# The last attention step: GpSimd subtracts the last head's probability remainders before three scatters instead of between them

## The chip, the cores and the metric

One core of a Trainium2 chip runs the whole kernel. Its engines work in parallel: TensorE (PE, with its weight loads as PEld), VectorE (DVE), ScalarE (ACT) and GpSimd (POOL); SyncE (SP) and GpSimd also issue DMA transfers. The metric is the device time of one execution in microseconds. Three runs of the kernel before gave 763.99, 764.95 and 767.49 us, so its median is 764.95 us.

## What is computed

Eight batches of eight attention heads (576 positions, 64 dimensions) are followed by a mixture of eight experts that picks one expert per token. Cut to what matters:

```python
scores = scale * np.matmul(q, k.transpose(0, 1, 3, 2))          # 8 x 8 heads, causal
bias = -(cum[:, :, :, None] - cum[:, :, None, :])               # from the running sum of s
scores = np.where(causal, -1000000000.0, scores + np.minimum(bias, 0.0))
attn = np.exp(scores - np.max(scores, axis=-1, keepdims=True))
attn = attn / (np.sum(attn, axis=-1, keepdims=True) + 1e-09)
x = np.matmul(attn, v)                                          # all heads of a token: 512 columns
...
expert_idx = np.argmax(logits, axis=1)                          # of normalised x and embeddings
for e in range(E):
    mask = expert_idx == e
    h = np.maximum(x[mask] @ w1[e], 0.0)
    out[mask] = gate_w[mask, None] * (h @ w2[e])
```

## The kernel before, in words

The attention part goes head by head, n = 0 to 63, one call of `step(n)` each. For a head TensorE computes the scores into the PSUM tiles `ta` and `tb`; ScalarE takes their exponentials into the f32 tile `P` (lines 498 and 501, columns 0 to 576 and 576 to 1600). A product in 16-bit needs each probability in two parts: the high one is the upper half of the f32 word, and the remainder `PL = P - high` is a subtraction that `pl_` writes, on GpSimd (helper `psub`, line 252) or, in some steps, partly on VectorE (line 508). `pv(n)` then multiplies high and remainder with the values into the one PSUM bank `om`: three matmuls per block, lines 526 to 528, of which line 528 reads `PL`. `norm1`, `norm2` and `norm3` (lines 539, 543 and 551, VectorE) divide and copy `om` into the token rows `xt`; the next `pv` writes `om` again and so waits for line 551.

`pv` runs one to two heads behind the scores. In the last step, n = 63, it has reached head 61; `pv` of heads 62 and 63 stand behind the loop, as does the second half of the last head's remainders.

When a batch of eight heads is done, its router ranks the tokens by expert, and five indirect DMAs (`scat`, line 670, called through `scatter()` from the queue `scats`) write the rows `xt` to the DRAM table `xs`, which is sorted by expert. GpSimd issues them. The five of batch 6, the batch preceding the last, stand in the last steps. Behind them GpSimd issues a gather `xload(0, 2)` (line 739), which reads the third tile of expert 0's rows back from `xs`; it waits for the last of these scatters to land. TensorE transposes the gathered tile in `xtr(0, 2)` (line 767).

TensorE does not wait for that: `first_pass(m)` (matmuls of line 903) multiplies the first 256 gathered rows with the eight 128-column pieces of expert 0's first weights. Behind the loop the order on TensorE is `pv(62)`, `first_pass(0)`, `pv(63)`, `first_pass(1)` to `first_pass(4)`, then `xtr(0, 2)` and `first_pass(5)` to `first_pass(7)`. The weights are made 16-bit in two parts as well: ScalarE writes the high part (line 875) and VectorE the low one (`wlow`, line 883, from two tiles in SBUF). Each `wlow` lets SP load another piece of weights (line 826).

The order on each engine is the order of the code: a manual schedule, in which an engine works through its own list and waits at semaphores. So the order of the calls in `step` and behind the loop is the order on GpSimd. Behind the loop stands:

```python
    for n in range(3, NH):
        step(n)
    pl_(NH - 1, 576, 1600, "p")
    while scats:
        scatter()
    xload(0, 2)
    pv(NH - 2, range(5))
    norms(NH - 2)
    wsq(15)
    wlow(1)
    first_pass(0)
    wsq(16)
    wlow(1)
    pv(NH - 1, range(5))
```

Of the kernel before, what the change touches and what calls it, by code (L numbers as in the profile page):

```python
# [31 lines left out]
SCN = [1, 1, 0, 0, 0, 0, 2, 1]  # L32
# [82 lines left out]
def main(ctx, tc, qkh, qkc, vtin, s_in, emb, tau, w1h, w2h, out, shared, nb):  # L115
# [36 lines left out]
    NH, LA = nb * H, 5  # L152
# [69 lines left out]
    def setup4():  # L222
        t = p2.tile([128, DM], F32, tag="lT", name="idx", bufs=1)
        for i, n in enumerate(("recf", "gp", "va", "gi", "tmp")):
            IX[n] = t[:, 40 * i:40 * i + 40].rearrange("p (b j) -> p b j", j=5)
        IX["cnt0"], IX["va0"], IX["gi0"] = t[:, 200:202], t[:, 202:205], t[:, 205:208].bitcast(I32)
        IX["gi"], IX["recf"], IX["va"], IX["va0"] = (IX[n].bitcast(I32) for n in ("gi", "recf", "va", "va0"))
        nc.gpsimd.iota(IX["recf"], pattern=[[S, 8], [128, 5]], base=0, channel_multiplier=1)
        nc.gpsimd.iota(IX["tmp"].bitcast(I32), pattern=[[NT, 8], [128, 5]], base=0, channel_multiplier=1)
        nc.gpsimd.tensor_copy(IX["gp"], IX["tmp"].bitcast(I32))  # L230
        IX["L"], IX["T"], IX["w"] = t[:, 284:324], t[:, 324:364], t[:, 364:369]
        IX["r"], IX["E"] = t[:, 224:244], t[:, 244:284]
        IX["WS"], IX["RS"], IX["SB"] = t[:, 432:434], t[:, 434:434 + 2 * NE], t[:, 450:454].bitcast(BF16)
        IX["SQ"] = t[:, 454:470].rearrange("p (k j) -> p k j", k=2)
        IX["b1"], one = t[:, 208:208 + NE], t[:, 216:216 + NE].bitcast(I32)
        nc.gpsimd.iota(one, pattern=[[NT, NE]], base=1, channel_multiplier=0)
        nc.gpsimd.tensor_copy(IX["b1"], one)
        zr = t[0:NE, 284:284 + XR // 4].bitcast(I32)
        nc.gpsimd.memset(zr, 0)
        for k in range(4):  # L240
            o = slice(XR // 4 * k, XR // 4 * (k + 1))
            nc.sync.dma_start(xs.rearrange("(e n) c -> e n c", e=NE)[:, 0, o], zr)
            nc.sync.dma_start(xs[0:SPM].rearrange("(t p) c -> t p c", p=128)[SPL // 128 - 1:, 127, o], zr[0:2])

    def setup3():
        nc.gpsimd.tensor_copy(base, ebase)
        nc.gpsimd.tensor_scalar(wsel, base, -1.0 / NT, float(NE), op0=ALU.mult, op1=ALU.add)
        nc.gpsimd.tensor_copy(wval, wsel.unsqueeze(1).to_broadcast([128, 5, NE]))
        nc.gpsimd.memset(wval[64:128, 4:5], 0.0)
# [4 lines left out]
    def load(g, o=slice(0, QW + KW)):  # L254
        if g >= NGg:
            return
        qkb = qkbs[g % 3]
        if g > 0:
            nc.gpsimd.dma_start(qkb[0:64, o], qkh[g][:, o], **(dict(max_dma_last_dim=4864) if g < 3 else {}))
        G[g] = dict(QB=qkb[:, 0:QW].rearrange("p (h s) -> p h s", h=HG), KB=qkb[:, QW:].rearrange("p (h s) -> p h s", h=HG))  # L260

    def loadc(g):
        if g == 1:
            for i in range(2):
                nc.gpsimd.dma_start(qkbs[1][64 + i:65 + i, QW:].bitcast(F32), chl[HG:2 * HG, i, :].bitcast(F32))
        elif 1 < g < NGg:
            nc.sync.dma_start(qkbs[g % 3][64:66, QW:].bitcast(F32), cumd[:, HG * g:HG * (g + 1), :].rearrange("x r s -> x (r s)").bitcast(F32))
# [45 lines left out]
    def hset(g):  # L313
        if g < NGg:
            for h in range(HG):
                HD.setdefault(HG * g + h, {}).update(QC=QCs[g % 2][:, h], KC=KCs[g % 2][:, h])
# [152 lines left out]
    def ta_(n, m):  # L469
        assert MP.get(("ready", n // 2))  # L470
        t = HD[n]["ta"] = ps_t.tile([128, 1024], F32, tag="t", name="ta")
        mask(t[:, 256:512], tri0, start=True)
        s1(m)
        hh_(n, t[:, 256:512], 0, 0, 256)
        hh_(n, t[:, 512:832], 0, 256, 576, True)
        hl_(n, t[:, 512:832], 0, 256, 576, True)
        hl_(n, t[:, 256:512], 0, 0, 256, True)
# [52 lines left out]
    def norm1(n):  # L530
        if n not in HD:
            return
        b, hh = n // H, n % H
        o = HD[n]["o"]
        if hh == 0:
            XT[b] = p2.tile([128, 5, XR], F32, name="xt", bufs=2)
        z = HD[n]["z"] = p2.tile([128, 5], F32, name="z")
        ov = HD[n]["ov"] = o[:, 0:365].rearrange("p (j c) -> p j c", c=73)
        nc.vector.tensor_scalar(z, ov[:, :, 72 * (hh % 2)], 1.0e-9 * 2.0 ** PSH, 2.0 ** XSH, op0=ALU.add, op1=ALU.mult)

    def norm2(n):
        if n in HD:
            nc.vector.reciprocal(HD[n]["z"], HD[n]["z"])
# [489 lines left out]
    def fslot():  # L1033
        while first:
            first.popleft()()  # L1035
# [151 lines left out]
    def step(n):  # L1187
        m = n + LA - (n < 6)
        live = n < NH
        b0, b1, c8 = n // H, n // H + 1, n % H  # L1190
        prev = n - 1 < NH
        g, c = n // HG, n % HG
        if live and c == 0:
            hset(g + 1)
            if n > 4:
                load(g + 2)
                loadc(g + 2)
        if n == 10:
            setup4()
            setup3()  # L1200
        fslot()
        norm1(n - 3)
        if live:
            ta_(n, m)
        if prev:
            pl_(n - 1, 576, PS(n), "p")
        sr(m, 3)
        norm2(n - 3)
        sa(m)
        if live:  # L1210
            expa(n)
            prep(n, True)
        norm3(n - 3)
        if NH - 7 < n < NH:
            brk[0] = False
            slots(4)
        if live:
            tb_(n)
        sr(m, 2)
        if live and n % 2 == 0:  # L1220
            tbm(n)
        s3(m)
        if live:
            if n % 2:
                tbm(n)
            tbl(n)
        if n < NH - 6 or n >= NH:
            mslot()
        if prev and PS(n) < 1600:
            pl_(n - 1, PS(n), 1600, "v")  # L1230
        if n < NH:
            wlow(1)
        k = n - NH + 8
        if k == 3:
            wsq(8, True)
        if n < NH - 1:
            emm(n)
        sb(n, m)
        sbr(m)
        if n < NH:  # L1240
            tail(n)
        if n == 5:
            s1(10)
            sr(10, 3)
            s2(10)
        if n == 7:
            vscale(1)
        pv(n - 2, [0, 1, 2])
        if n == 7:
            fslot()  # L1250
        if rq:
            rq.popleft()()
        if n == 5:
            sr(10, 2)
            sr(10, 1)
            s3(10)
        pv(n - 2, [3, 4])
        if n == NH - 1:
            emm(n)
        if n == 5:  # L1260
            s4(10)
        if NH - 7 < n < NH:
            mslot()
        if n >= NH - 1:
            for f in (norm1, norm2, norm3):
                f(n - 2)
        if live:
            expb1(n)
            if k == 7:
                wsq(13)  # L1270
            vcp(n, False)
        if k == 3:
            wsum(0)
        aslot()
        if n == 4:
            load(3)
            loadc(3)
        if live:
            prep(n, False)
            vcp(n, True)  # L1280
        if n == NH - 1:
            xcv(0, 0)
            xtr(0, 1, pxs())
            xcv(0, 1)
        if k > 0:
            wsq((0, 2, 5, 8, 9, 10, 11, 14)[k])
            wcv((0, 0, 0, 0, 2, 1, 2, 1, 1, 1, 0)[k], True)
        brk[0] = False
        if n < NH - 6:
            slots(4)  # L1290
        if n in (4, 5, 6):
            vsq(1, ((0,), (1, 2), (3,))[n - 4])
        if H <= n < NH and 2 <= c8 < 6 and b1 < nb:
            vsq(b1, (c8 - 2,))
        if live and c8 == 6 and 1 < b1 < nb:
            vscale(b1)
        if n == 3:
            loadt(1, pair(1))
        if H <= n < NH and c8 < 4:
            loadt(b1, c8)  # L1300
        if n == NH - 9:
            wissue(3)
        for _ in range(SCN[c8] if n < NH - 22 else 2 if NH - 3 < n < NH else 1 + (c8 > 5) + 4 * (n > NH - 6)):
            scatter()
        later()
        if live and c == 0:
            addl(g + 1, True)
        if live and c == 1:
            addl(g + 1, False)
        mrow1(m)  # L1310
        if live:
            pl_(n, 0, 576, "p")

    def PS(n):
        return 1024 if NH - 7 < n < NH - 1 else 1600
# [390 lines left out]
```

## Time and profile before

| | |
|---|---|
| median of three runs | 764.95 us (763.99 to 767.49) |
| profiled execution, its own time | 763.98 us |
| its span, first to last instruction | 762.3 us |
| busy: PE / DVE / ACT / POOL | 97% / 70% / 75% / 52% of the span |
| PE waits over 0.15 us between 335 and 375 us | 0.18, 0.92, 0.34 and 5.94 us |

A busy share is an average over the whole span. The change is in one stretch of it, from about 335 to 351 us, where the attention part ends and the experts begin; there it is the single waits of the engines that count, and the time at which each comes. A row of the timeline gives the start in us from the span's start, the duration in us, the engine, the line, the operation, what it writes and reads, its shape, and in brackets the idle time of the engine before it with what ended it. The time of a transfer is not in the row of its issue: a DMA row gives the time that the engine took to issue it.

### The profile page before, as it was taken

How to read it: one execution, taken by the hardware profiler on the slowest of the kernel's cores; microseconds unless marked ns; L12 is line 12 of the kernel's file. 1: busy time of each engine (PE TensorE's matmuls, PEld its weight loads, DVE VectorE, ACT ScalarE, POOL GpSimd, SP SyncE). 2: the span in 40 equal slices, each digit the busy share in tenths (PEclk: the TensorE clock that was granted, in tenths of full speed). 3: DMA queues.
4: the chain of work that ended last, by engine and by line, in shares of the span. 5: the costliest groups of instructions: out<-in, count | busy, mean ns of one | idle time of the engine just before them, and what ended most of it. 6: DMA issues, size and time to landing. Idle time of an engine off the chain costs nothing. (4 is left out here: it accounts for less than half of the span.)

```text
span 762.3 us, 20951 instructions
## 1 busy us (share of the span) xinstructions
PE 739.1 (97%) x7992; PEld 536.4 (70%) x7992; DVE 530.2 (70%) x1818; ACT 568.2 (75%) x1029; POOL 397.2 (52%) x376
## 2 busy tenths in 40 slices
PE   7999999999999999999689999999999999999996
PEld 4889999999999999998365455545444554554554
DVE  8778888888888888898467767655665566745621
ACT  9898989898989998986377867837648578475410
POOL 9997898989897989693422113222221122312011
PEclk9999999999999999999899999999999999999999
DMA  7789879797979796874525956845755668553001
GB/s 151 175 193 191 173 180 204 180 207 168 216 172 210 181 215 155 174 256 132 172 89 168 207 171 194 159 139 152 181 171 141 177 186 186 169 130 100 13 15 58
DMA packets 76003, 124.01 MB, mean 163 GB/s; under 512 B 38824, under 2 KB 39232, under 8 KB 75033
## 3 DMA queue, kind: packets, MB, share of 16 engines
q0 software_dynamic: 19632, 69.69, 39.4%
q1 hardware_dynamic: 56260, 52.84, 25.9%
q8 instruction: 71, 1.16, 0.7%
q14 instruction: 40, 0.32, 0.1%
HBM read 93.99 MB, written 21.49 MB: 151 GB/s over the span
## 5 line engine op out<-in xcount | busy, mean ns | idle before, releaser
L252 POOL TENSOR_TENSOR PL<-P 128x576 f16<-128x576 f32 (+2 forms) x128 | 205.6, 1726 | 13.1 <-ACT P L498 8.6
L903 PE MATMUL pe<-xH,wt 128*128 128x512 f16 (+1 forms) x576 | 153.1, 344 | 0.5 <-PEq L1008 0.5
L982 POOL DMA_INDIRECT out<-Kx,xj x39 | 43.2, 1108 | 195.0 <-DVE Kx L981 164.5
L903 PEld LDWEIGHTS <-wt 128*128 128x128 f16 x960 | 86.0, 98 | 80.8 <-issue 1.5
L526 PE MATMUL om<-vh,P 128*128 128x73 f16 x960 | 106.9, 199 | 0.5 <-DVE sc L1035 0.3
L528 PE MATMUL om<-vh,PL 128*128 128x73 f16 x960 | 106.1, 197 | 0.9 <-POOL PL L252 0.9
L527 PE MATMUL om<-vl,P 128*128 128x72 f16 x960 | 106.3, 196 | 0.0
L739 POOL DMA_INDIRECT Qx<-xs,idx x40 | 46.5, 1163 | 108.3 <-ACT vjunk L838 41.3
L362 PE MATMUL s<-qkb 96*128 96x288 f32 (+4 forms) x272 | 96.2, 368 | 2.0 <-DVE M L370 0.9
L903 PE MATMUL pe<-xL,wt 128*128 128x512 f16 (+1 forms) x288 | 96.0, 344 | 0.0
L527 PEld LDWEIGHTS <-P 128*128 128x128 bf16 x960 | 94.7, 99 | 0.9 <-issue 0.5
L528 PEld LDWEIGHTS <-PL 128*128 128x128 f16 x960 | 93.8, 98 | 1.0 <-POOL PL L252 1.0
L526 PEld LDWEIGHTS <-P 128*128 128x128 bf16 x960 | 93.8, 99 | 0.6 <-DVE xt L551 0.4
L905 PE MATMUL pxs<-xH,wt 128*128 128x64 f16 x432 | 83.2, 193 | 0.0
L370 DVE CUSTOM_DVE_ANT_0 junk<-s,mS 128x448 bf16<-128x448 f32 (+3 forms) x144 | 73.9, 520 | 5.0 <-PE s L362 3.1
L974 PE MATMUL pxs<-wt,hq 128*128 128x512 f16 x297 | 74.0, 384 | 0.0
L501 ACT ACTIVATE P<-tb 128x1024 f32<-128x1024 f32 x64 | 65.2, 1018 | 3.0 <-PE tb L467 1.9
L974 PEld LDWEIGHTS <-hq 128*128 128x128 f16 x360 | 35.5, 99 | 42.7 <-issue 1.7
L905 PEld LDWEIGHTS <-wt 128*128 128x128 f16 x648 | 63.5, 98 | 0.4
L464 PE MATMUL tb<-QC,KC 128*128 128x448 f32 (+3 forms) x256 | 63.4, 307 | 0.0
L460 PE MATMUL tb<-qkb 128*128 128x448 f32 (+3 forms) x256 | 61.1, 286 | 0.0
L883 DVE SCALAR_TENSOR_TENSOR wt<-ring,idx,wt 128x512 f16<-128x512 f32 x80 | 56.8, 745 | 4.7 <-ACT wt L875 4.6
(328 smaller groups left out, 1997.3 us busy)
## 6 DMA issues: line engine op xcount, KB each, us to landing
qkb<-qkh POOLq DMA_DIRECT2D x15, 1216.0 KB, 8.9
ring<-w2h SPq DMA_DIRECT2D x44, 256.0 KB
ring<-w1h SPq DMA_DIRECT2D x36, 256.0 KB
KC<-qkh POOLq DMA_DIRECT2D x14, 576.0 KB, 8.5
QC<-qkh POOLq DMA_DIRECT2D x14, 576.0 KB, 9.1
vT<-vtin SPq DMA_DIRECT2D x24, 320.0 KB
rw<-w1h SPq DMA_DIRECT2D x15, 256.0 KB
rw<-w2h SPq DMA_DIRECT2D x12, 256.0 KB
```

The lines of the kernel that those rows point to most:

```text
L252: nc.gpsimd.tensor_tensor(out, a, b_, op=ALU.subtract)
L362: nc.tensor.matmul(out, G[g]["QB"][0:96, h, 128 * i:128 * i + 128], G[g]["KB"][0:96, h, lo:hi], start=True, stop=True)
L370: nc.vector.tensor_tensor_reduce(out=jk, in0=src, in1=ms, scale=1.0, scalar=NEG, op0=ALU.add, op1=ALU.max, accum_out=MP[n // 2][:, n % 2, ...
L460: nc.tensor.matmul(out, G[g]["KB"][:, h, ks:ks + 128], G[g]["QB"][:, h, 64 + qlo:64 + qhi], start=start, stop=False)
L464: nc.tensor.matmul(out, HD[n]["KC"][:, ks:ks + 128], HD[n]["QC"][:, qlo:qhi], start=False, stop=stop)
L501: nc.scalar.activation(HD[n]["P32"][:, 576:1600], HD[n]["tb"], AF.Exp, scale=0.125)
L526: nc.tensor.matmul(out, lh, vh[:, kb], start=(kb == 0), stop=False)
L527: nc.tensor.matmul(out[:, u:u + 72], lh, vl[:, kb], start=False, stop=False)
L528: nc.tensor.matmul(out, ll, vh[:, kb], start=False, stop=(kb == j))
L903: nc.tensor.matmul(h, w[:, 128 * c:128 * c + 128], x[:, c, lo:hi], start=(c == 0 and k == 0), stop=(c == 3 and k == 2))
L905: nc.tensor.matmul(X["a"][:, HALF * m:HALF * m + HALF], w[:, 128 * c:128 * c + 128], x[:, c, hi:hi + HALF], start=(c == 0 and k == 0), sto ...
L974: nc.tensor.matmul(y, h, w, start=(m == 0 and k == 0), stop=(m == 7 and k == 2))
```

## The change

In step n = 63 the loop that calls `scatter()` no longer runs, where it ran twice before; in step 62 it still runs twice. The two scatters stay in the queue `scats`, and the `while scats` behind the loop now issues three instead of one, after both halves of the last head's remainders.

```diff
-        for _ in range(SCN[c8] if n < NH - 22 else 2 if NH - 3 < n < NH else 1 + (c8 > 5) + 4 * (n > NH - 6)):
+        for _ in range(SCN[c8] if n < NH - 22 else 2 if n == NH - 2 else 0 if n == NH - 1 else 1 + (c8 > 5) + 4 * (n > NH - 6)):
             scatter()
```

On GpSimd the list changes in one place, the last step of the attention part. `PL2` and `P322` belong to head 62, `PL0` and `P320` to head 63; `xs` is the table in DRAM, `Qx` the tile that the gather fills.

```order
 L252 TENSOR_TENSOR PL2_112<-P322_88 128x576
 L252 TENSOR_TENSOR PL2_112<-P322_88 128x1024
-L670 DMA xs_61<-xt_5631,pos_6704 36864x580 x2
-L252 TENSOR_TENSOR PL0_110<-P320_86 128x576
-L252 TENSOR_TENSOR PL0_110<-P320_86 128x1024
-L670 DMA xs_61<-xt_5631,pos_6704 36864x580
+L252 TENSOR_TENSOR PL0_110<-P320_86 128x576
+L252 TENSOR_TENSOR PL0_110<-P320_86 128x1024
+L670 DMA xs_61<-xt_5631,pos_6704 36864x580 x3
 L739 DMA Qx_6608<-xs_61,idx_1290 128x580
 L554 COPY xt_6488<-idx_1290 128x5x4
```

The two subtractions of head 63 move up past two scatters, and now follow those of head 62 directly; all three scatters stand together ahead of the gather.

VectorE's list is the same before and after. Around the same place it holds these rows (the first `L883` is the `wlow` of step 63; the first three rows behind it are the norm of head 61, the next three that begin with `L539` the norm of head 62):

```order
L883 SCALAR_TENSOR_TENSOR wt<-rw_177,idx,wt 128x512
L539 TENSOR_SCALAR z<-om 128x5
L543 RECIPROCAL z<-z 128x5
L551 TENSOR_TENSOR xt<-om,z 128x5x72
L311 SCALAR_TENSOR_TENSOR vl<-V,sc,vh_109 128x2x144
L777 TENSOR_TENSOR rv<-pxs,xH 128x4x128 x2
```

Nothing moves in it; what changes is which of GpSimd's instructions run beside it.

## Rows read from the trace of the kernel before

**Rows 1.** The page: span, and busy time of each engine.

```profile
span 762.3 us, 20951 instructions
PE 739.1 (97%) x7992; PEld 536.4 (70%) x7992; DVE 530.2 (70%) x1818; ACT 568.2 (75%) x1029; POOL 397.2 (52%) x376
```

**Rows 2.** Waits, 325 to 374 us: total, times, longest, in us.

```profile
PE om L528 <- POOL PL L252: 0.9, 1, 0.9
PE pxs L767 <- DMA Qx<-xs,idx: 0.3, 1, 0.3
```

**Rows 3.** Timeline of PE: heads 62 and 63, the passes, both transposes.

```profile
339.81 0.21 PE L526 MATMUL om<-vh,P 128*128 128x73 f16 x1 [0.18 <-DVE xt L551]
...
342.78 0.20 PE L526 MATMUL om<-vh,P 128*128 128x73 f16 x1
...
344.13 0.21 PE L528 MATMUL om<-vh,PL 128*128 128x73 f16 x1 [0.92 <-POOL PL L252]
...
350.55 0.27 PE L903 MATMUL h<-xH,wt 128*128 128x256 f16 x1
...
351.16 0.30 PE L767 MATMUL pxs<-ident,Qx 128*128 128x128 f32 x1 [0.34 <-DMA Qx<-xs,idx]
...
374.39 0.48 PE L767 MATMUL pxm<-ident,Qx 128*128 128x128 f32 x1 [5.94 <-DMA Qx<-xs,idx]
```

**Rows 4.** Timeline of POOL: remainders of heads 62 and 63, three scatters, gather.

```profile
335.30 1.18 POOL L252 TENSOR_TENSOR PL<-P 128x576 f16<-128x576 f32 x1
336.40 1.92 POOL L252 TENSOR_TENSOR PL<-P 128x1024 f16<-128x1024 f32 x1
338.49 1.26 POOL L670 DMA_INDIRECT xs<-xt,pos  x1 [0.17 <-issue]
340.06 0.98 POOL L670 DMA_INDIRECT xs<-xt,pos  x1 [0.31 <-issue]
341.05 3.02 POOL L252 TENSOR_TENSOR PL<-P 128x576 f16<-128x576 f32 x2
344.24 1.20 POOL L670 DMA_INDIRECT xs<-xt,pos  x1 [0.17 <-issue]
347.49 1.04 POOL L739 DMA_INDIRECT Qx<-xs,idx  x1 [2.05 <-DMA xs<-xt,pos]
```

**Rows 5.** Timeline of ACT: the last exponential of head 63.

```profile
336.76 1.02 ACT L501 ACTIVATE P<-tb 128x1024 f32<-128x1024 f32 x1 [0.25 <-POOL PL L252]
```

**Rows 6.** Timeline of DVE: three low weights, and one norm copy.

```profile
330.17 1.64 DVE L883 SCALAR_TENSOR_TENSOR wt<-rw,idx,wt 128x512 f16<-128x512 f32 x1
...
335.78 3.10 DVE L883 SCALAR_TENSOR_TENSOR wt<-rw,idx,wt 128x512 f16<-128x512 f32 x1
...
341.94 0.53 DVE L551 TENSOR_TENSOR xt<-om,z 128x360 f32<-128x360 f32 x1
342.39 2.23 DVE L883 SCALAR_TENSOR_TENSOR wt<-wt,idx 128x512 f16<-128x512 f32 x1
```

**Rows 7.** Timeline of POOL: earlier remainders, one alone and two in a row.

```profile
317.03 0.94 POOL L252 TENSOR_TENSOR PL<-P 128x448 f16<-128x448 f32 x1 [1.08 <-ACT P L501]
...
329.74 1.52 POOL L252 TENSOR_TENSOR PL<-P 128x576 f16<-128x576 f32 x1 [0.40 <-ACT P L498]
331.22 1.38 POOL L252 TENSOR_TENSOR PL<-P 128x448 f16<-128x448 f32 x1
```

**Rows 8.** Timeline of SP: the first of three weight loads from 338.94.

```profile
338.94 0.33 SPq L826 DMA_DIRECT2D rw<-w1h  x1
```

**Rows 9.** Timeline of POOL: the last of five later scatters, and its gather.

```profile
364.44 0.99 POOL L670 DMA_INDIRECT xs<-xt,pos  x1 [0.30 <-issue]
370.93 1.05 POOL L739 DMA_INDIRECT Qx<-xs,idx  x1 [5.50 <-DMA xs<-xt,pos]
```

**Rows 10.** Windows: busy by engine and instructions, TensorE clock, DMA share, GB/s.

```profile
344.50:347.50 3.00, 3.00 (x53) 2.78 (x50) 2.96 (x11) 0.57 (x2) 0.95 (x2) 1.00 0.28 68
363.00:369.50 6.50, 5.45 (x26) 2.25 (x23) 5.17 (x28) 2.79 (x10) 2.12 (x2) 1.00 0.83 277
```

## The prediction

> **What bounds the kernel now.** I read the page first: TensorE is busy for 97% of a span of 762.3 us [rows 1], so time is won or lost only where TensorE waits or starts to wait. The list of waits for the stretch around the change comes next, and shows two kinds that touch it [rows 2]: one wait of line 528 for GpSimd's remainders, and one of the transpose, line 767, for the gathered tile. The timeline of TensorE puts them in order [rows 3]. pv(62) starts at 339.81, released by VectorE's norm of head 61. pv(63) starts at 342.78, stops almost at once, and goes on at 344.13, after an idle 0.92 us that GpSimd's last subtraction ended. The passes then run without a gap up to 350.55 + 0.27 = 350.82, and the transpose waits 0.34 us for the gather and starts at 351.16. The reader is to see that the two waits are 7 us apart, and that nothing but TensorE's own work lies between them.
>
> GpSimd's timeline says why each ends when it does [rows 4]. The remainders of head 63 start at 341.05, after two scatters, and end at 344.07. The third scatter starts at 344.24, the gather 3.25 us later, at 347.49, when that scatter has landed, and TensorE's transpose 3.67 us after the gather's start. So both waits hang on the same engine, and the change shortens one by moving work that stands ahead of the other.
>
> **The change, part by part.**
>
> The subtractions. Nothing else holds them back: the second exponential of head 63 ends at 336.76 + 1.02 = 337.78 [rows 5], before GpSimd has finished head 62 at 336.40 + 1.92 = 338.32 [rows 4]. The two take 3.02 us together, so undisturbed they end at 338.32 + 3.02 = 341.3, and pv(63) at 342.78 finds them ready. The stop in pv(63) goes: about 1.0 us (0.92 us of idle time in the row, and a few matmul slots of a tenth beside it).
>
> The scatters. Their number and the number of subtractions ahead of the gather are the same as before. Undisturbed the third would start 341.3 + 0.17 after the subtractions, then two intervals as before: 340.06 - 338.49 = 1.57 for the first and 0.98 + 0.31 = 1.29 for the second, at 344.3 against 344.24 [rows 4]. The gather then stays where it was, within 0.1 us.
>
> The neighbour on VectorE. A low weight of line 883 starts at 335.78 and takes 3.10 us; it ends 0.56 us after GpSimd's 338.32. The one at 342.39 ends at 344.62, 0.55 us after GpSimd's 344.07 [rows 4, 6]. So line 883 makes no progress beside a subtraction of GpSimd, while the norm copy of line 551 at 341.94 keeps its 0.53 us. In the changed list the first of them finds another subtraction waiting at 338.3 where there was a scatter. The rows show both outcomes of such a meeting. At 330.17 line 883 waits for a subtraction that ends at 331.26, gets in ahead of the next, which stands in the row from 331.22 and takes 1.38 us instead of 0.94, and ends at 331.81 [rows 6, 7]. At 336.40 the next subtraction came first, and VectorE waited through both [rows 4, 6].
>
> I take the first outcome, since the two rows overlap by 0.04 us where VectorE got in and by 0.08 us where it did not (335.30 + 1.18 against 336.40), and the boundary at 338.3 has a wide subtraction in front, whose successor is the narrower one, as at 331.2 the successor was narrow. It is one case each, so I keep the other as a rival. The price of the first is 1.38 - 0.94 = 0.44 us on GpSimd: the subtractions end at 341.3 + 0.44 = 341.7, still a microsecond before pv(63), and the third scatter starts at 344.75, 0.5 us later than before. With 3.25 and 3.67 us behind it as before, the transpose starts at 344.75 + 6.92 = 351.67 instead of 351.16.
>
> The Trainium skill states a rule for this meeting (SBUF — State Buffer, Who interferes with whom): VectorE and GpSimd share one pair of ports as an exclusive lock, a VectorE instruction with two SBUF inputs needs it, and whoever issues first has it for the whole instruction. By that rule VectorE, waiting since 335.78, would get the pair at the first boundary, and the slow outcome could not occur. The row of 3.10 us disagrees, since it spans two subtractions, and the measurement decides: both outcomes stay open.
>
> What is late next. TensorE arrives at the transpose 1.0 us earlier, at 349.8, and the tile arrives 0.5 us later: it waits 1.8 us there instead of 0.34. All of the gain is given back there, and 0.5 us more. From then on everything hangs on TensorE: the passes 5 to 7, and behind them the ranks and the scatters of the last batch. So the 5.94 us at 374.39 [rows 3] absorb nothing, because the gather that ends them comes later by the same amount.
>
> The sum: -1.0 for the stop in pv(63), +1.0 for the earlier arrival at the transpose, +0.5 for the later gather: +0.5 us. Against the profiled execution's own 763.98 us that is 764.5. The median of the runs is 0.97 us above that execution, so 765.5 us as a median of runs. From below, with VectorE's turn free, the term is +0.1; from above it is the first rival.
>
> **The rivals.**
>
> VectorE is shut out through both pairs, and the kernel gets slower. Place: the boundary at 338.3. If GpSimd's next subtraction comes first there, as it did at 336.40, and again at 339.4, line 883 ends at 341.3 + 0.56 = 341.8 instead of 338.88, 2.95 us later. Behind it in VectorE's list stands the norm of head 61, and pv(62) waits for that: 342.76 instead of 339.81. The stop of pv(63) is gone, so TensorE is 2.95 - 1.0 = 1.95 us late, ends the passes at 352.8, finds the tile landed, and is 1.6 us behind 351.16: 766.6. The three weight loads from 338.94 [rows 8] follow line 883 and move into the scatters' time, which can add another 1.0 us. It decides from the point at which line 883 ends more than 1.9 us later than now. For it: the row of 3.10 us; against it: the row of 1.64 us. Should VectorE get in at 339.4, between the two subtractions of head 63, the norm is 1.1 us late, the removed stop pays for that, and the sum stays at +0.5.
>
> The three scatters hinder each other. The last of five scatters in a row starts at 364.44, and the gather behind it at 370.93, 6.5 us later against 3.25 here [rows 4, 9]. If three in a row cost as much, the transpose comes another 3.25 us later, +3.8 in all: 768.7. Against it: DMA was busy for 0.83 of the time there and for 0.28 behind the third scatter here [rows 10], and the weight loads that fill the difference are not issued in this place.
>
> The stop goes and most of it stays gone. This needs the gather to land a microsecond earlier than now, or the tile not to be needed; the row of the transpose with its 0.34 us shows that it was already the later of the two, so at most 0.3 us is free of that condition. For it: two of GpSimd's idle gaps beside scatters could close, 0.17 and 0.31 us. Price: -0.3 to -1.0, so 764.0 to 764.7.
>
> The change does not do what it says, because the subtractions wait for the exponential: excluded by 337.78 against 338.32, down to a delay of 0.5 us of ScalarE.
>
> **How the numbers follow.** The forecast, given back at the transpose with +0.1 to +0.8, has a chance of 0.58; VectorE shut out 0.21; scatters that hinder each other 0.09; a gain kept 0.09; anything else 0.03. The predicted time is 765.5 us. The forecast's own range is 764.2 to 767.0, since a median of three runs of this kernel moves by more than its term: the runs before lie between 763.99 and 767.49. With the shut-out VectorE at 766.6 to 767.6 and half of the kept gain, the range is 763.4 to 768.1. About 0.5%, 3.8 us here, is what a measurement of this kernel can tell from no change: faster would be below 761.1 and slower above 768.8. No case reaches the first, and the scatters' case reaches the second only with some help. So 0.02 faster, 0.94 within, 0.04 slower.
>
> **What would show it.** Right: line 528 of head 63 without a wait for GpSimd; line 883 ending near 338.9; the third scatter near 344.7 and the gather near 348.0; TensorE's wait at the transpose grown from 0.34 to about 1.8 us. The first rival shows as a row of line 883 of about 6 us and a wait of 3 us at the first matmul of pv(62), with almost none at the transpose; the second as a gather that starts over 5 us after the third scatter; the third as a transpose that starts before 351. A time below 763 or above 768.8 would make the prediction wrong as a whole.

## The result: slower by 0.6%, outside the predicted range

| | us |
|---|---|
| predicted | 765.5 (763.4 to 768.1) |
| after, median of five runs | 771.61 (771.43 to 772.53) |
| before, median of five runs in the same comparison | 766.24 (763.99 to 767.49) |
| ratio, 95% interval | 1.0063 [1.0046, 1.0080] |
| the same comparison on another chip | 1.0044 [1.0027, 1.0061] |

Medians and ratios here and below are over the fast executions; two that were far slower, 1056.04 us of before and 4257.9 us of before with one low weight put off, are left out.

The profiled execution of after took 771.61 us. Its page, beside [rows 1]: the span is 7.5 us longer, TensorE is busy 4.2 us longer (at a lower clock, as will be seen), and VectorE 4.2 us longer with the same 1818 instructions.

```profile
span 769.8 us, 20951 instructions
PE 743.3 (97%) x7992; PEld 539.1 (70%) x7992; DVE 534.4 (69%) x1818; ACT 568.0 (74%) x1029; POOL 395.5 (51%) x376
```

The waits of TensorE from 325 to 374 us of after (total, times, longest), beside [rows 2]: the stop of line 528 and the wait at the transpose are both gone, and a new wait of 4.9 us stands where there was none, at line 526.

```profile
PE om L526 <- DVE xt L551: 4.9, 1, 4.9
PE V L300 <- DVE vl L311: 0.4, 1, 0.4
PE om L526 <- DVE base L641: 0.3, 1, 0.3
```

TensorE's timeline of after, beside [rows 3]. The wait is at the first matmul of pv(61), one head earlier than any place the prediction spoke of. pv(62) starts at 347.67 and pv(63) at 350.62, without a stop. The row of 357.41 is the third tile's transpose, which starts without a wait, 6.25 us later than before.

```profile
337.49 0.60 PE L767 MATMUL pxs<-ident,Qx 128*128 128x128 f32 x4
...
343.00 0.22 PE L526 MATMUL om<-vh,P 128*128 128x73 f16 x1 [4.92 <-DVE xt L551]
...
346.82 1.01 PE L767 MATMUL pxs<-ident,Qx 128*128 128x128 f32 x4
347.67 0.20 PE L526 MATMUL om<-vh,P 128*128 128x73 f16 x1
...
350.62 0.20 PE L526 MATMUL om<-vh,P 128*128 128x73 f16 x1
...
357.41 0.60 PE L767 MATMUL pxs<-ident,Qx 128*128 128x128 f32 x4
```

GpSimd's timeline of after, beside [rows 4]. The four subtractions are one row now, 5.97 us without a pause, and end at 340.95; the third scatter is 0.28 us earlier than before, and its gather follows 5.87 us later instead of 3.25.

```profile
333.99 0.99 POOL L670 DMA_INDIRECT xs<-xt,pos  x1 [0.30 <-issue]
334.98 5.97 POOL L252 TENSOR_TENSOR PL<-P 128x576 f16<-128x576 f32 x4
341.12 1.26 POOL L670 DMA_INDIRECT xs<-xt,pos  x1 [0.17 <-issue]
342.68 0.98 POOL L670 DMA_INDIRECT xs<-xt,pos  x1 [0.30 <-issue]
343.96 0.93 POOL L670 DMA_INDIRECT xs<-xt,pos  x1 [0.30 <-issue]
349.83 1.04 POOL L739 DMA_INDIRECT Qx<-xs,idx  x1 [4.93 <-DMA xs<-xt,pos]
```

VectorE's timeline of after, beside [rows 6], says what TensorE waited for. The low weight of **step 62** starts at 334.70 and takes 6.81 us: it ends 0.56 us after the last of the four subtractions. Behind it stands the norm of head 60, whose copy of line 551 releases pv(61). The low weight of step 63, about which the prediction was, comes at 342.87 and takes 0.74 us.

```profile
334.70 6.81 DVE L883 SCALAR_TENSOR_TENSOR wt<-rw,idx,wt 128x512 f16<-128x512 f32 x1
341.43 0.66 DVE L311 SCALAR_TENSOR_TENSOR vl<-V,sc,vh 128x432 f16<-128x432 f32 x1
342.01 0.15 DVE L539 TENSOR_SCALAR z<-om 128x5 f32<-128x5 f32 x1
342.19 0.19 DVE L543 RECIPROCAL z<-z 128x5 f32<-128x5 f32 x1
342.42 0.53 DVE L551 TENSOR_TENSOR xt<-om,z 128x360 f32<-128x360 f32 x1
342.87 0.74 DVE L883 SCALAR_TENSOR_TENSOR wt<-rw,idx,wt 128x512 f16<-128x512 f32 x1
```

Two windows of after (columns as in [rows 10]) show the second part of the price: after the wait began, TensorE's granted clock was 0.50 of full speed, 1.2 instead of 2.4 GHz, for 6.83 us, and once more for 3.42 us after a 1.91 us wait at 401.6. The execution before had a wait of 1.83 us in that later place, too, but no fall of the clock behind it.

```profile
340.82:347.65 6.83, 4.65 (x53) 4.60 (x53) 3.65 (x10) 0.58 (x2) 3.30 (x4) 0.50 0.68 199
402.26:405.68 3.42, 3.42 (x9) 1.18 (x8) 2.66 (x18) 2.70 (x7) 0.00 (x0) 0.50 0.29 87
```

**The sum against the profile of before.** The transposes of the first and second gathered tile start 2.52 us apart before (336.51 and 339.03) and 9.33 apart after. Of the 6.81 more, 4.92 is the wait, and the other 1.9 the halved clock. The first transpose itself was 0.98 us late already. Behind that 1.54 us are saved, the stop (about 1.0) and the waits at the transpose (0.34) and at pv(62) (0.18), so the third tile is 0.98 + 6.81 - 1.54 = 6.25 us late. The rest of the 7.5 us of span comes later, with the second fall of the clock: the two transposes around it (401.57 and 408.96) stand 7.39 us apart, the same two 5.70 us in before (395.73 and 401.43). That fall cannot be put down to the change. The same two transposes are 7.38 us apart in before with both low weights put off, and 5.70 in after with a memset added (both follow below).

The 0.98 us are not the change's doing. They arise at 325.1, ten microseconds ahead of the first moved instruction, where VectorE's share of a remainder (line 508) meets a subtraction of GpSimd. The timelines of VectorE and GpSimd there, first of before, then of after:

```profile
325.13 0.74 DVE L508 TENSOR_TENSOR PL<-P 128x576 f16<-128x576 f32 x1
...
322.49 4.17 POOL L252 TENSOR_TENSOR PL<-P 128x448 f16<-128x448 f32 x3
```

```profile
325.13 1.53 DVE L508 TENSOR_TENSOR PL<-P 128x576 f16<-128x576 f32 x1
...
322.50 3.54 POOL L252 TENSOR_TENSOR PL<-P 128x448 f16<-128x448 f32 x3
```

In the one profile of before VectorE went first (0.74) and GpSimd waited; here GpSimd went first and VectorE took 1.53. In all twelve other profiles of this study it went as here. TensorE then waits 0.34 us at line 526 (for line 641) and 0.41 us at line 300 (for line 311), both for VectorE, where it did not wait in the first profile of before; that is most of the 0.98 us.

### The profile page after: what moved, and what is told of

The parts are those of the page before. It is cut to its first block, busy times and chain, and to the rows that moved or that the text cites. A ratio compares the mean times of both kernels' runs of the same rounds, so it can differ in the third digit from the quotient of the medians.

```text
span 769.8 us, 20951 instructions
## 1 busy us (share of the span) xinstructions
PE 743.3 (97%) x7992; PEld 539.1 (70%) x7992; DVE 534.4 (69%) x1818; ACT 568.0 (74%) x1029; POOL 395.5 (51%) x376
## 5 line engine op out<-in xcount | busy, mean ns | idle before, releaser
L883 DVE SCALAR_TENSOR_TENSOR wt<-ring,idx,wt 128x512 f16<-128x512 f32 x80 | 56.8, 745 | 4.8 <-ACT wt L875 4.8
```

## The experiments

The theory: VectorE's line 883 has two inputs in SBUF and makes no progress beside a subtraction of GpSimd, nor at the boundary between two of these that follow each other directly. A scatter between the pairs ended its wait; the change took that scatter away. Rivals: that the three scatters together make the time, or the clock alone. Starts are those of the transposes of tiles 0 to 3 on TensorE.

| kernel | line 883, step 62 / 63 | longest wait, tile 0 to 1 | starts of tiles 0, 1, 2, 3 | span | median; ratio to before |
|---|---|---|---|---|---|
| before, first profile | 0.74 / 3.10 | none | 336.51, 339.03, 351.16, 374.39 | 762.3 | 766.24 |
| before, second profile | 3.87 / 0.74 | 1.99 | 338.20, 343.94, 354.52, 378.49 | 768.0 | 769.58; 0.9992 |
| after | 6.81 / 0.74 | 4.92 | 337.49, 346.82, 357.41, 380.76 | 769.8 | 771.61; 1.0063 |
| after, second profile | 6.81 / 0.74 | 4.91 | 337.58, 346.92, 357.50, 380.95 | 770.1 | 770.39; 1.0044 |
| after, one scatter between | 3.87 / 3.10 | 1.98 | 338.47, 344.64, 355.34, 379.34 | 768.4 | 769.48; 1.0012 |
| after, memset between | 6.86 / 0.74 | 4.96 | 338.25, 347.07, 357.61, 381.12 | 770.9 | 773.67; 1.0050 |
| after, both low weights late | none there | none | 337.77, 340.28, 352.78, 375.89 | 763.2 | 765.36; 0.9985 |
| before, both low weights late | none there | none | 338.03, 340.54, 353.09, 375.94 | 765.0 | 765.87; 0.9986 |

Before was run beside each set: 768.51 for the first (35 runs), 766.98 for the second (29), 769.75 for the third (20) and 766.91 for the last (22). Its times differ by nearly as much between the sets as the effect asked for, so the ratios are what is compared. One difference between the sets shows in the traces: every profile of the first and third sets has a wait of 2.51 to 3.78 us at line 974 for line 883, and no other profile has it. What makes it was not tried.

**First set: does it hang on the low weights, on the scatter or on the clock?** Both low weights of steps 62 and 63 are put off to a place behind pv(63), in after and in before. This changes part of the computation: a few low parts of expert 0's first weights are made from raw weights that the next ones have already replaced.

```diff
-        if n < NH:
+        if n < NH - 2:
             wlow(1)
...
-    wlow(4)
+    wlow(6)
```

> The changed kernel, with the low weights of steps 62 and 63 (line 883, two tiles in SBUF as inputs) put off until after the attention steps, so that none of them stands beside the four subtractions. Lock theory (VectorE's instruction waits as long as GpSimd's subtractions follow each other, and the norm of head 61 waits behind it): TensorE's wait of 4.92 us at pv(61) falls below 0.5 us, its clock stays at 2.4 GHz around 341 to 348 us, and the time is 763 to 766.5 us, about 5 to 8 us below the changed kernel. Scatter theory (three scatters in a row make the gather late, and that costs the 5 us): the gather still starts 5.9 us after the third scatter, and the time stays at 770 to 772.

> The kernel before, with the low weights of steps 62 and 63 put off in the same way: what the putting off is worth by itself. Lock theory: before loses little to the lock, since a scatter separates the two pairs of subtractions; the stop of 0.92 us in pv(63) stays, and the time is 763 to 766. A theory in which the putting off itself is worth the 5 us: 760 to 762.

After with this took 771.16 us, ratio 1.0030 [1.0013, 1.0048]; before with it 769.44, 1.0005 [0.9990, 1.0021]. Both times miss the lock theory's ranges, and that of after lies in the scatter theory's. The place did what the lock theory says: in after the first two transposes stand 2.51 us apart, the wait of pv(61) is gone, and the gather starts 2.98 us after the third scatter, not 5.9. In before the stop in pv(63), which I expected to stay, did not come; TensorE waited 1.57 us at pv(62) instead. Passes on TensorE waited for low weights (0.35 and 0.48 us at line 903, 3.75 and 3.78 at line 974, all for line 883). The waits at line 903 stand in these two kernels alone; that at line 974 is the one of the whole set, so the putting off makes at most a part of it. After also had a wait of 2.55 us at pv(63), ended by the norm of head 62; what held that norm its records leave open. By the total the test is inconclusive; the second set mends it.

One scatter goes back between the pairs:

```diff
-2 if n == NH - 2 else 0 if n == NH - 1 else
+2 if n == NH - 2 else 1 if n == NH - 1 else
```

> The changed kernel with one of the three scatters back between the subtractions of head 62 and those of head 63; two follow behind. Lock theory: VectorE gets in at that scatter, the low weight that waited 6.81 us waits at most 4 us, and the time is 764 to 768. Scatter theory: two scatters in a row instead of three delay the gather by a third less, 769 to 770.5.

It took 769.48 us, 1.0012 [0.9994, 1.0031]: by the ratio most of the loss is gone. The time itself lies in the range of the scatter theory; the ranges were set from 766.24 us for before, which took 768.51 in this set. In the timelines of VectorE and GpSimd line 883 of step 62 ends 0.56 us after the first pair, beside the scatter that follows, and takes 2.94 us less than in after; that of step 63 then waits beside the second pair. The gather starts 6.32 us after the second of the two scatters (5.87 after the third of three in after), so the scatter theory fails here.

```profile
335.69 3.87 DVE L883 SCALAR_TENSOR_TENSOR wt<-rw,idx,wt 128x512 f16<-128x512 f32 x1
...
340.91 3.10 DVE L883 SCALAR_TENSOR_TENSOR wt<-rw,idx,wt 128x512 f16<-128x512 f32 x1
...
335.98 3.02 POOL L252 TENSOR_TENSOR PL<-P 128x576 f16<-128x576 f32 x2
339.17 1.26 POOL L670 DMA_INDIRECT xs<-xt,pos  x1 [0.17 <-issue]
340.45 3.00 POOL L252 TENSOR_TENSOR PL<-P 128x576 f16<-128x576 f32 x2
```

The clock by itself: 22 matmuls without use fill TensorE's wait in after.

```diff
+        if n == NH - 1:
+            for _ in range(22):
+                w = wt(1, 0)[0]
+                nc.tensor.matmul(HD[n]["ta"][:, 512:1024], w[:, 0:128], w, start=True, stop=True)
         pv(n - 2, [0, 1, 2])
```

> The changed kernel with 22 matmuls of 512 columns into a part of ta that nothing reads, ahead of pv(61), where TensorE waits 4.92 us: 4.7 us of work in the time of the wait. Lock theory with a term for the clock: the wait for VectorE ends at the same time, near 343, but the granted clock stays at 2.4 GHz, and what stood at 1.2 GHz (heads 61's products, the second transpose) gets its 1.9 us back: 769 to 770. If the clock is no part of the loss: 771 to 772.5.

It took 770.89 us, 1.0029 [1.0010, 1.0047], between the two ranges, and the total cannot be told from that of after (1.0044 [1.0027, 1.0061]), which was not run in this set. Line 883 still took 6.81 us, and these windows show the clock at 1.00 where after had 0.50. The first three tiles' transposes start at 338.62, 346.21 and 357.33. The first two are 7.59 us apart against 9.33: the clock's part of the price is 1.74 us there. Of these 1.21 are left at the third tile (18.71 us after the first, against 19.92), since TensorE now waits 0.91 us at pv(62). The lock's part stays.

```profile
340.80:344.20 3.40, 3.23 (x17) 1.42 (x16) 3.33 (x6) 0.46 (x2) 2.92 (x3) 1.00 0.10 30
344.20:347.60 3.40, 2.61 (x53) 2.44 (x53) 1.37 (x5) 0.83 (x2) 1.53 (x2) 1.00 1.00 279
```

**Second set: the low weights moved with the whole computation kept.** The two go to the place just ahead of pv(63), which is behind the subtractions; beside it, the one of step 62 alone (there `n < NH and n != NH - 2`, and `wlow(2)`), and after unchanged.

```diff
-        if n < NH:
+        if n < NH - 2:
             wlow(1)
...
     wsq(16)
-    wlow(1)
+    wlow(3)
     pv(NH - 1, range(5))
```

> The changed kernel itself again, beside the others of this set on one chip. All theories: 5 us (0.6%) over before, with the low weight of step 62 waiting through four subtractions, 6.8 us, and a wait of about 5 us on TensorE at pv(61).

> The changed kernel with the low weights of steps 62 and 63 issued after the norm of head 62 instead, three in a row there, so that all weights are ready where they were and only VectorE's order differs. Lock theory: no wait over 0.3 us at pv(61), pv(62) and pv(63); the second transpose follows the first after 2.5 us instead of 9.3; then the gather is the later one, and the third transpose follows the second after 11.5 to 13 us; 5 to 7 us below after2, so within 0.3% of before. Scatter theory: as after2.

> The kernel before with the same putting off. Lock theory: before loses up to 2.5 us to the lock in some runs (the row of 3.10 us), so 0 to 2 us below before; the stop in pv(63) stays. If the putting off costs or gives something by itself, it shows here alike: more than 2 us either way.

> The changed kernel with only the low weight of step 62 put off; that of step 63 stays and comes after the norm of head 60, at about 336.5. Lock theory: it then waits from there to the end of the four subtractions, some 4.5 us instead of 6.8; the norm of head 61 is late, not that of head 60: TensorE waits about 2.5 us at pv(62) and not at pv(61), the first rival as it was predicted; 2 to 3 us below after2. A theory in which only the total of VectorE's work counts: as after2.

After unchanged repeats its profile to a tenth (6.81, 4.91). With both put off it takes 765.36 us (764.63 to 767.20), 0.9985 [0.9971, 0.9999], 5.0 us less than after beside it; its lead on before is at the edge of what can be told. Its GpSimd still does four subtractions and three scatters in a row, so neither the scatters nor the order of GpSimd by itself cost the time. From the first tile to the third TensorE waits only for the third, for which the row of its timeline is:

```profile
352.78 0.63 PE L767 MATMUL pxs<-ident,Qx 128*128 128x128 f32 x4 [1.80 <-DMA Qx<-xs,idx]
```

Before with the same takes 765.87 us, 0.9986 [0.9971, 1.0001]. The stop in pv(63) that I expected to stay is not there: pv(63) starts at 344.29, and head 63's last subtraction ends at 344.02. The third tile's transpose waits 1.84 us. So with line 883 out of the way the change has no stop to save, and is worth nothing that can be measured (765.36 against 765.87).

With step 62's alone put off after takes 765.66 us, 0.9984 [0.9973, 0.9995]. I had expected 2 to 3 us below after, and it was 4.7. Line 883 of step 63 waits through the boundaries that are left, and TensorE waits at pv(62), 1.84 us and not the expected 2.5. That takes the place of the 1.80 us for the third tile, and no clock falls.

```profile
337.13 4.82 DVE L883 SCALAR_TENSOR_TENSOR wt<-rw,idx,wt 128x512 f16<-128x512 f32 x1
...
342.88 0.21 PE L526 MATMUL om<-vh,P 128*128 128x73 f16 x1 [1.84 <-DVE xt L551]
```

**Third set: before once more, and a small gap.**

> The kernel before, unchanged, for a second profile. If its first profile was the usual course: VectorE's line 883 of step 62 takes about 0.75 us, that of step 63 about 3.1, and pv(63) stops for 0.9 us at its first line 528. If that profile was one of two courses (GpSimd lost the port to VectorE at 325.1 there, and has won it in every profile since), VectorE comes about 1 us later, line 883 of step 62 meets GpSimd's pair of head 62 and takes about 3 us, TensorE comes up to 1 us later to pv(63) and does not stop there, and waits 1.8 us or more at the transpose of the third tile. Time: 1.0 within 0.2% of the runs of before either way.

The second profile of before took the other course. Line 508 took 1.53 us, VectorE came later, and it was step 62's line 883 that met head 62's pair; the scatter at 338.90 let it in. TensorE waited 1.99 us at pv(61), its clock fell (the window's 0.52), pv(63) did not stop, and contrary to what I expected there was no wait for the third tile, since TensorE was later still. Rows of VectorE, TensorE and a window:

```profile
325.84 1.53 DVE L508 TENSOR_TENSOR PL<-P 128x576 f16<-128x576 f32 x1
...
335.42 3.87 DVE L883 SCALAR_TENSOR_TENSOR wt<-rw,idx,wt 128x512 f16<-128x512 f32 x1
...
340.78 0.19 PE L526 MATMUL om<-vh,P 128*128 128x73 f16 x1 [1.99 <-DVE xt L551]
...
341.50:344.90 3.40, 3.40 (x39) 3.33 (x36) 1.07 (x4) 0.72 (x2) 3.23 (x3) 0.52 0.92 268
```

Against this course the change reads simply: line 883 takes 6.81 - 3.87 = 2.94 us longer, TensorE waits 4.92 - 1.99 = 2.93 us longer, and the clock takes 1.9 instead of 1.2 us (9.33 and 5.74 us between the first transposes, less 2.51 and the wait). That is 3.6 us, where the comparisons measured 5.4 and 3.4. Which course each run of before took, its time does not tell.

Then a memset of 128x8, which reads nothing, between the two pairs in after:

```diff
             scatter()
+        if n == NH - 1:
+            nc.gpsimd.memset(const.tile([128, 8], F32, name="gap"), 0.0)
         later()
```

> The kernel after, with one small instruction more on GpSimd between the subtractions of head 62 and those of head 63: a memset of 128x8, which reads nothing. Theory (VectorE is kept out as long as GpSimd's subtractions follow each other without a gap, whatever else differs): the memset opens a gap, line 883 of step 62 ends about 1 us after head 62's second subtraction, as it did at the scatter in the run with one scatter (3.9 us instead of 6.8), TensorE's wait at pv(61) falls from 4.9 to about 2 us, and the time is 2 to 4 us below the kernel after. Rival (only an instruction that leaves the port for a microsecond, as a scatter does, lets VectorE in, or the memset needs the port itself): line 883 still takes 6.8 us or more, TensorE waits 4.9 us, and the time is that of the kernel after, within 0.2%.

It took 773.67 us, 1.0050 [1.0030, 1.0071], as slow as after. The signs are the rival's: the memset of 0.13 us lets nobody in, as VectorE's row beside GpSimd's shows. But it opened no gap. The first pair's row ends at 338.77, after the memset has begun, and the second pair's begins at 338.75, before the memset ends. So the theory of the gap is not refuted by this run, and what a gap without an instruction would do was not tried.

```profile
335.75 3.02 POOL L252 TENSOR_TENSOR PL<-P 128x576 f16<-128x576 f32 x2
338.69 0.13 POOL L1306 MEMSET gap<- 128x8 f32 x1
338.75 3.01 POOL L252 TENSOR_TENSOR PL<-P 128x576 f16<-128x576 f32 x2
...
335.45 6.86 DVE L883 SCALAR_TENSOR_TENSOR wt<-rw,idx,wt 128x512 f16<-128x512 f32 x1
```

**Fourth set: the prediction's own meeting.** With the low weight of step 61 alone put off (`n < NH and n != NH - 3`, `wlow(2)`) VectorE comes to step 62 early, as in the first profile of before.

> The kernel after, with the low weight of step 61 alone put off until shortly before pv(63). VectorE then comes to step 62 about a microsecond earlier, as in the first profile of the kernel before, so that the meeting comes about that the prediction spoke of: line 883 of step 62 passes before head 62's subtractions (0.75 us), and line 883 of step 63 stands at the boundary between the pairs of heads 62 and 63. The prediction's step (VectorE gets in at that boundary): line 883 of step 63 takes about 2.5 us, no wait at pv(62), the time that of the run in which both low weights were put off, 5 us below the kernel after. Its first rival with the mechanism found since (kept out until the last subtraction): line 883 of step 63 takes about 5 us and ends near 341.9, TensorE waits about 2 us at pv(62), and most of that only replaces the wait for the third tile: 4 to 5 us below the kernel after, at most 1 above the run with both put off.

> The kernel before with the same low weight put off. Both theories: line 883 of step 62 takes 0.75 us, that of step 63 about 3 us and gets in at the scatter behind head 62's pair, the 2.0 us wait at pv(61) that the second profile of before showed is gone, the stop of pv(63) at its first line 528 comes back (0.5 to 0.9 us). Time 1 to 3 us below the kernel before.

After with this takes 766.0 us, 0.9989 [0.9973, 1.0006]; before with it 765.29, 0.9978 [0.9963, 0.9993]. Step 62's line 883 passes in 0.74 us in both. In after that of step 63 waits across the boundary inside head 62's pair, across the one between the pairs, on which the prediction rested, and across the one inside head 63's pair:

```profile
334.64 5.96 POOL L252 TENSOR_TENSOR PL<-P 128x576 f16<-128x576 f32 x4
...
335.63 5.54 DVE L883 SCALAR_TENSOR_TENSOR wt<-rw,idx,wt 128x512 f16<-128x512 f32 x1
...
342.09 0.21 PE L526 MATMUL om<-vh,P 128*128 128x73 f16 x1 [2.55 <-DVE xt L551]
```

In before it takes 2.61 us and ends behind the scatter's start; pv(63) stops for 0.35 us, and the third tile's transpose waits 1.13 us, for a router step on VectorE (line 623). Its ratio is the lowest of all, but not clear of the others that lie below 1.

## Why the prediction was wrong, step by step

- **The stop of pv(63) goes.** Right in after: no wait of line 528. But the stop was there only in the course of the first profile (0.92 us); in the second there was none, in before with both low weights put off there was none either, and with step 61's put off it was 0.35. So the term of -1.0 was there in one profile of before only.
- **"I take the first outcome", VectorE gets in at the boundary at 338.3.** This step failed: a price of 0.44 us on GpSimd was set for it, and in after VectorE stayed out at that boundary and at both others, for 6.81 us, and TensorE waited 4.92 us for what stands behind. In ten profiles line 883 stood waiting at boundaries between these four subtractions, 21 in all, and it got in at none. Even in the meeting that the prediction described (5.54 us, step 61's put off) it lost all three. Of the two reasons given, the width of the successor is refuted: between the pairs a 1024-wide one is followed by a 576-wide one, and in the five profiles in which line 883 waited there, it did not get in. The other reason, the overlap of the rows, is taken up in the last section.
- **Which instruction meets the burst.** It was step 62's line 883, which starts ahead of the first subtraction, and so waits through four of them, not through what is left from 335.78 on. Behind it stands the norm of head 60 and pv(61), not head 61's and pv(62). The prediction took the place of one execution, in which VectorE had won a meeting at 325.1, for the place of all; in the other thirteen profiles VectorE lost that meeting.
- **The first rival** had the mechanism and named its signs: a row of about 6 us (6.81), a wait of 3 us (4.92), almost none at the transpose. With step 61's put off its signs came in the place that it named, too: 5.54 us, 2.55 at pv(62), and 0.21 at the transpose, for line 619. Its price of +1.6 was too small in after for two reasons: the instruction was the earlier one, which waits longer and blocks an earlier norm, and the clock was not priced (1.74 to 1.9 us at this place). Against that, part of both is lost in the second course of before as well.
- **The scatters.** The third started at 343.96 instead of 344.75, since GpSimd lost nothing at the boundary. The gather came 5.87 us behind it, not 3.25, so the scatters' rival came near the size (it had 6.5), though not by its cause: 6.32 us stand behind two scatters in a row, 2.98 behind three. TensorE reached the tile at 357.41 and nothing waited for it. With both low weights put off the distance was 4.61 us, and the wait at the transpose 1.80. That is the forecast's "about 1.8" by luck: before, without the change, waits 1.84 there.
- **The fourth tile absorbs nothing.** Right: after waits 6.1 us there where before waited 5.94, and its transpose is 6.37 us later.
- **The sum.** Where step 61's low weight is put off, the two kernels differ by 766.0 - 765.29 = 0.71 us, near the +0.5 that was forecast. That is luck: it came by other steps, and the intervals of the two ratios overlap, so the two kernels cannot be told apart.

Not settled: when the clock falls, and for how long. A wait of 1.99 us at pv(61) was followed by a fall in the second profile of before, waits of 1.84 and 2.55 us at pv(62) by none (1.00 from 340 to 345 us with step 62's or step 61's low weight put off), and one of 2.55 us at pv(63), in after with both put off behind pv(63), by a fall again (0.59 from 347 to 350 us). A wait of 4.9 us was followed by 6.83 us at half in after, and one of 4.96 us in the kernel with the memset by about 3.4 (its clock is 0.76, 0.50 and 0.89 in the windows of 2 us from 342). Nor is the fall at 402 explained, which follows a wait that other executions have without it.

## What to carry to other kernels

Ahead of moving work on one engine, look for what its neighbour does in the gaps that the move closes: the DMA issues between GpSimd's pairs of subtractions were the only moments in this place in which VectorE could finish an instruction with two SBUF inputs, and behind that instruction stood the norm that TensorE needed. A burst is priced by the whole queue behind the instruction that it blocks, and a wait of some microseconds on TensorE by the clock that it may lose, which cost over a third as much again here. Where two engines race for something, one profile shows one outcome: look for the same meeting elsewhere in the trace, and price both courses of the kernel before as well as of the kernel after.

## What the runs showed of the hardware

- **A blocked VectorE instruction can wait through several GpSimd instructions.** Line 883 took 0.74 us alone, 3.87 through two subtractions and 6.81 to 6.86 through four. The Trainium skill (SBUF — State Buffer, Who interferes with whom) has the port pair locked for a whole instruction, by whoever issues first. Alone that rule would let the waiting VectorE in at the first boundary; these rows show that it is not so. Nor does an earlier start help: in the six profiles in which line 883 of step 62 waited, its record begins some 0.3 us ahead of GpSimd's first subtraction.
- **What differs at the boundaries.** By their starts and ends in ns, the records of one subtraction and the next overlap by 0.054 to 0.079 us at the 21 boundaries where line 883 stayed out. At the earlier boundaries, from a 576-wide to a 448-wide one, the overlap is 0.031 to 0.040 us wherever VectorE got in, and 0.041 to 0.044 in the thirteen profiles in which line 508 did not get in at 325. So the order by overlap that the prediction gave as its first reason holds, though at the earlier boundaries by 1 ns only, and GpSimd's spans are rough. The long overlaps are also no sign of the contest: the same boundaries have 0.055 to 0.076 us in the four kernels with both low weights put off, where no line 883 stood waiting. So whether the overlap decides, or only goes with the widths, is open.
- **A scatter lets VectorE in, a small memset does not:** 1.26 us against 0.13 us of GpSimd's time. GpSimd's record is idle for 0.17 us ahead of such a scatter, and not ahead of or behind the memset; and line 883 ends 0.56 us after the last subtraction, whether 2 or 4 went before. Whether the idle time, the length or the kind of the instruction decides is open.
- **From a scatter to the gather that waits for it** it took 2.98 to 6.32 us in this one place: 3.25, 4.15, 4.61 and 5.87 in before, after with step 61's low weight put off, after with both put off ahead of pv(63), and after. In the five profiles with 5.87 us and more, the last three weight loads (line 826) start between 1.13 us before the last scatter and 0.61 us after it; in none of the other nine do all three start there. DMA was busy for 0.28 of the time behind that scatter in before [rows 10] and for 0.68 of the first window of after above; that the weight loads are the cause was not tried by itself.
